# Global attention's transposes four blocks a bank in a row, the diagonal block last and copied with the others of its bank

## The chip, the cores and the metric

The kernel runs on one core of one Trainium2 chip, in one launch. The metric is the device time in microseconds of that core; lower is better. TensorE (PE) multiplies matrices, its weight loads are shown apart (PEld); VectorE (DVE), ScalarE (ACT) and GpSimd (POOL) work on elements; SyncE (SP) and ACT issue the transfers from memory here. TensorE writes its results to PSUM, which this kernel uses as eight banks of 128 x 512 single-precision values, and DVE or ACT copy them from there to the on-chip memory (SBUF) in which operands lie.

## The reference

Three layers follow each other, for 4 batches of 576 positions:

```python
# 1. attention of 8 heads (width 64) in a window of 64 positions
mask = (rel >= 0) & (rel < 64)
x = softmax(where(mask, q @ k.T / 8, -1e9)) @ v
# 2. four experts, each a causal attention of width 64 over all 576 positions
for e in range(4):
    q, k, v = x @ wq[e], x @ wk[e], x @ wv[e]
    a = softmax(where(causal, -1e9, q @ k.T / 8))
    out += weight_e * (a @ v @ wo[e])     # weight_e: softmax over the best 2 of 4 gates, else 0
# 3. mixing over positions, then over channels
theta = x @ w_theta
y = w_tok_r @ (x * cos(theta)) + w_tok_i @ (x * sin(theta))
u = x + y
return u + maximum(u @ w_ch, 0)
```

## The kernel before

The kernel is written as Python generators, one for each piece of work on a batch, and `merge` (line 45) interleaves them by costs from the table `KN` (line 27): at each turn the piece with the smallest share of its cost done goes on. That gives each instruction its rank. The framework's scheduler then sets the final order of each engine's queue, sets all waits, and lets buffers of a pool take turns. Each engine works its queue strictly in that order.

`phase_a` is the windowed attention (its tiles are `as`, `ams`, `apt`, `ao`). `qk` and `vg_gates` make the experts' queries, keys, values and gates (`qk`, `vg`). `attn(b, ep)`, line 403, is the global attention that the change touches: batch `b`, experts `2*ep` and `2*ep + 1` (a pair). `wo` projects its result (`x2`), `theta`, `mix` and `channel` are layer 3 (`th`, `xk`, `y`, `c`). Products are made of three matmuls each of split operands (`mm3`, lines 93 to 95).

`attn` takes five row tiles, t = 0 to 4; tile t has t full blocks of 128 columns and a diagonal block of 64 columns for each expert. For each expert of the pair:

- scores on TensorE into a bank `bs` (lines 432 and 434), mask and minimum on DVE (436), exp on ACT in place (441), sums and reciprocal on DVE (445, 446);
- scaling by DVE or POOL (453): the off-diagonal part in place in `pn` (traced as `bms`), the diagonal block into `pd` (`bpd`, both experts side by side).

Then, after a `yield`, TensorE transposes: off-diagonal blocks j = 0 .. t-1, for both experts each, two values of j (four transposes) a bank `bpt` (lines 458 to 464), and the diagonal block, both experts at once, in a bank of its own `bdt` (469, 470). Each bank is copied to `pT` (`bpT`) by ACT or DVE (466 and 468; 472 and 474). `KN["BC"]` = [1, 0, 1, 1] and `KN["BD"]` = [2, 1, 2, 1] choose the engine by batch. The products `o` read `pT`: off-diagonal ones from the last j down to 0 (480; traced at lines 145 and 148), the diagonal one with weights `VD` last (482). ACT and DVE split the result into `oh` and `ol` (483; traced at 87 and 90).

The banks `bpt`, `bdt` and `o` all come from `tbank` (line 399): two buffers that take turns (`tb`); in the last batch every third request goes to another bank (`ta`). A bank can be written again once all readers of its last tile are done. Over the five tiles a pair of experts asks for 1, 2, 2, 3 and 3 banks for transposes and one a tile for `o`, 16 in all.

Layers 1 and 2 of different batches run interleaved up to some 302 us; the middle of the span, from 64 us, is where the global attention runs.

Of the kernel before, what the change touches and what calls it, by code (L numbers as in the profile page):

```python
# [21 lines left out]
P = 128  # L22
# [35 lines left out]
def kernel(ctx, tc, qT, kT, vw, consts, w_in, w_o, w_th, w_tk, w_ch, outT):  # L58
    nc = tc.nc
# [5 lines left out]
    ident, ma1, ma0 = (cst[:, P * i : P * i + P] for i in range(3))  # L65
# [12 lines left out]
    def bank(shape, tag, name):  # L78
        return ps.tile(shape, F32, tag=tag, bufs=BANKS[tag], name=name)

    def pool_mul(out, in_, by):
        nc.gpsimd.tensor_scalar(out=out, in0=in_, scalar1=by, scalar2=1.0,  # L82
                                op0=ALU.mult, op1=ALU.mult)

    def split(dst_h, dst_l, src, eng_h, eng_l):
        if eng_h is nc.scalar:
            nc.scalar.copy(out=dst_h, in_=src)  # L87
        else:
            eng_h.tensor_copy(out=dst_h, in_=src)
        eng_l.tensor_sub(out=dst_l, in0=src, in1=f32(dst_h))  # L90
# [49 lines left out]
    def together():  # L140
        first = []

        def product(out, w, x, **flags):
            if not first:
                first.append(nc.tensor.matmul(out, w, x, **flags))
            else:
                with tc.issue_after(first[0].ins), tc.high_priority():
                    nc.tensor.matmul(out, w, x, **flags)

        yield product  # L150
# [29 lines left out]
    def sums(kind, tiles):  # L180
        nsum[kind] += 1
        return tiles[nsum[kind] % 4]
# [212 lines left out]
    def sbank(b, shape, name):  # L395
        ns[0] += 1
        return bank(shape, "as" if b == B - 1 and ns[0] % KN["SB"] == 0 else "bs", name)

    def tbank(b, shape, name):
        nt[0] += 1  # L400
        return bank(shape, "ta" if b == B - 1 and nt[0] % KN["TB"] == 0 else "tb", name)

    def attn(b, ep):
        vg, gw = VG[b], GW[b]
        for i in range(2):
            e = 2 * ep + i
            pool_mul(VD[ep][64 * i : 64 * i + 64, :, i, :], vg[0:64, :, e * D : (e + 1) * D], 1.0)
        oh = bp.tile([P, S], F32R, tag="oh", bufs=3, name=f"oh{b}{ep}")
        ol = bp.tile([P, S], F32R, tag="ol", bufs=3, name=f"ol{b}{ep}")
        O[b, ep] = (oh, ol)  # L410
        for t in range(5):
            w = QW[t]
            q0 = 0 if t == 0 else 64 + P * (t - 1)
            m = 64 if t == 0 else P
            mo = S - P if t == 0 else S - w
            if b == B - 1 and ep == 1 and t % 3 == 1:
                pn = rp.tile([P, 2, S], F32, tag="bmsx", name=f"bms{b}{ep}{t}")
            else:
                pn = bp.tile([P, 2, S], F32, tag="bms", bufs=2, name=f"bms{b}{ep}{t}")
            ss = sums(1, BS)  # L420
            sm = bp.tile([P, 2], F32, tag="bsm", bufs=4, name=f"bsm{b}{ep}{t}")
            pd = bp.tile([P, 2, 64], F32, tag="bpd", bufs=2, name=f"bpd{b}{ep}{t}")
            for i in range(2):
                e = 2 * ep + i
                n = f"{b}{e}{t}"
                qs, ka = QS[b, e], KA[b, e]
                ms = pn[:, i]
                cuts = [(0, w)] if w <= 512 else [(0, w // 2), (w // 2, w)]
                nm = bp.tile([P, 2], F32, tag="bnm", bufs=6, name=f"bnm{n}")
                for ci, (a, z) in enumerate(cuts):  # L430
                    s = sbank(b, [P, 512], f"bs{n}{a}")
                    nc.tensor.matmul(s[:m, : z - a], qs[:, q0 : q0 + m], ka[:, a:z],
                                     start=True, stop=False)
                    nc.tensor.matmul(s[:m, : z - a], qs[:, q0 : q0 + m], KL[e][:, a:z],  # L434
                                     start=False, stop=True)
                    nc.vector.tensor_tensor_reduce(  # L436
                        out=ms[:m, a:z], in0=s[:m, : z - a], in1=mb[:m, mo + a : mo + z],
                        scale=-0.125, scalar=nm[:m, 0:1] if ci else 3.0e38,
                        op0=ALU.add, op1=ALU.min, accum_out=nm[:m, ci : ci + 1],
                    )  # L440
                ex = nc.scalar.activation(out=ms[:m, :w], in_=ms[:m, :w], func=AF.Exp,  # L441
                                     bias=nm[:m, ci : ci + 1], scale=-1.0, accum_out=ss[:m, i, 0:1])
                if (b, ep, t, i) == (3, 1, KN["LT"], 1):
                    late[0] = ex
            nc.vector.tensor_reduce(out=sm[:m], in_=ss[:m], op=ALU.add, axis=AX.X)
            nc.vector.reciprocal(out=sm[:m], in_=sm[:m])
            for i in range(2):
                eng = nc.gpsimd if (False, i == 1 and t < 4, i == 1, t >= 2, i == 1 or t >= 3, True)[KN["SC"][2 * b + ep]] else nc.vector
                ms = pn[:, i]
                for dst, src in ((pd[:m, i], ms[:m, P * t : w]), (ms[:m, : P * t], ms[:m, : P * t])):  # L450
                    if src.shape[1] == 0:
                        continue
                    eng.tensor_scalar(out=dst, in0=src, scalar1=sm[:m, i : i + 1],
                                      scalar2=gw[:m, t, 2 * ep + i : 2 * ep + i + 1],
                                      op0=ALU.mult, op1=ALU.mult)
            yield 0.25 * (t + 1)
            pT = bp.tile([P, 5, 2, P], F32, tag="bpT", bufs=2, name=f"bpT{b}{ep}{t}")
            for j0 in range(0, t, 2):
                jn = min(2, t - j0)
                pt = tbank(b, [P, 2, 2, P], f"bpt{b}{ep}{t}{j0}")  # L460
                for jj in range(jn):
                    j = j0 + jj
                    for i in range(2):
                        nc.tensor.transpose(pt[:, jj, i, :], pn[:, i, P * j : P * j + P], ident)  # L464
                if (0, j0 == 2, t % 2, 1)[KN["BC"][b]]:
                    nc.vector.tensor_copy(out=pT[:, j0 : j0 + jn], in_=pt[:, :jn])
                else:
                    nc.scalar.copy(out=pT[:, j0 : j0 + jn], in_=pt[:, :jn])
            pt = tbank(b, [P, P], f"bdt{b}{ep}{t}")
            nc.tensor.transpose(pt[:, :m], pd[:m].rearrange("p h d -> p (h d)"), ident[:m, :m])  # L470
            if KN["BD"][b] == 0 or KN["BD"][b] == 1 and t % 2:
                nc.vector.tensor_copy(out=pT[:, t, 0, :m], in_=pt[:, :m])
            else:
                nc.scalar.copy(out=pT[:, t, 0, :m], in_=pt[:, :m])
            o = tbank(b, [P, P], f"o{b}{ep}{t}")
            for f in together():
                for j in reversed(range(t)):
                    for i in range(2):
                        e = 2 * ep + i
                        f(o[64 * i : 64 * i + 64, :m], vg[:, j, e * D : (e + 1) * D],  # L480
                          pT[:, j, i, :m], start=(j == t - 1), stop=False)
            nc.tensor.matmul(o[:, :m], VD[ep][:, t].rearrange("p h d -> p (h d)"), pT[:, t, 0, :m], start=(t == 0), stop=True)
            split(oh[:, q0 : q0 + m], ol[:, q0 : q0 + m], o[:, :m], nc.scalar, nc.vector)
            yield 0.4 * (t + 1)
# [169 lines left out]
    for i in range(2):  # L654
# [3 lines left out]
          (KN["CW"][5], load_w(w_in[:, W0:], NC, lambda c: wih[:, c, W0:], lambda c: wil[:, c, W0:], "bms")))  # L658
    for b in range(B):
        todo = [(KN["AT"][2 * b], attn(b, 0)), (KN["QK"][2 * b], qk(b, 1))]  # L660
        if KN["WOI"] == 2 * b:
            todo.append((KN["CW"][6], load_w(w_o, 2, lambda c: woh[c], lambda c: wol[c], "zc")))
# [16 lines left out]
        if b == 3:  # L679
# [4 lines left out]
            wkh += [kp.tile([P, S], F32R, name=f"wkh{c}") for c in range(NK0, 9)]  # L684
            wkl += [kp.tile([P, S], F32R, name=f"wkl{c}") for c in range(NK0, 9)]
        todo = [(KN["AT"][2 * b + 1], attn(b, 1))]
        if b < B - 1:
            todo += [(KN["QK"][2 * b + 1], qk(b + 1, 0)), (KN["VG"][b + 1], vg_gates(b + 1))]
# [88 lines left out]
```

## Time and profile before

| what | us |
|---|---|
| median of 3 runs | 528.98 (528.73 to 529.41) |
| the profiled execution | 528.16 |
| its span, from first to last instruction | 526.4 |
| TensorE busy | 506.6 |
| ACT busy | 329.6 |
| DVE busy | 323.1 |
| POOL busy | 304.6 |

The profile is of one execution. Busy time is time with an instruction of the program in work; for TensorE the ends of matmuls are modelled, so short waits between them can hide in it. The granted clock of TensorE is 1.00 (2.4 GHz) in every stretch. Rows name lines of the kernel and tiles without their numbers; `out<-in` are the tiles written and read, the shape after it partitions by elements, and a bracket shows how long the engine sat idle before, and what ended that.

### The profile page before, as it was taken

To read this page: it belongs to the slowest core of one execution; us is meant where nothing else is said; L and a number is where in the kernel's file an instruction comes from. 1 tells how busy PE (TensorE), PEld (TensorE's weight loads), DVE (VectorE), ACT (ScalarE), POOL (GpSimd) and SP (SyncE) were. 2 spreads that over 40 slices of the span, in tenths; PEclk is the share of its full clock that TensorE was granted. 3 is DMA by queue.
4 is the path that set the end of the run, shared out by engine and by line. 5 is a ranking of instruction groups with operands and counts; after the bars stand their busy time and mean duration, and the time that the engine had idled before them with its cause. 6 is when DMAs were issued, how large, how long until landed. Compare 5 with 4: busy or idle time off the path is not lost.

```text
span 526.4 us, 12343 instructions
## 1 busy us (share of the span) xinstructions
PE 506.6 (96%) x4372; PEld 475.5 (90%) x4372; DVE 323.1 (61%) x1244; ACT 329.6 (63%) x1045; POOL 304.6 (58%) x464
## 2 busy tenths in 40 slices
PE   8879999999999999999998999999999999999997
PEld 6669888899998998989787998999999999999997
DVE  5876887858778597558988787553325324533312
ACT  7977698866878768677788977551437136523410
POOL 5798789664848842247876676951475226531420
PEclk9999999999999999999999999999999999999999
DMA  7865224222314421112004121002000200011002
GB/s 248 253 185 169 97 60 147 64 67 92 103 34 134 142 76 32 32 29 73 37 2 159 62 82 42 1 0 80 12 2 1 68 24 1 1 57 35 1 1 91
DMA packets 21086, 36.80 MB, mean 70 GB/s; under 512 B 2336, under 2 KB 13600, under 8 KB 21024
## 3 DMA queue, kind: packets, MB, share of 16 engines
q1 hardware_dynamic: 19008, 31.22, 18.7%
q10 hardware_dynamic: 2016, 4.79, 2.7%
q8 instruction: 35, 0.57, 0.5%
q14 instruction: 27, 0.22, 0.2%
HBM read 31.28 MB, written 4.72 MB: 68 GB/s over the span
## 4 chain that ended last, share of the span: by engine, by line
PE 70%; DVE 11%; ACT 6%; POOL 6%; issue 3%; DMA 3%; ACTq 0%; POOLq 0%; DVEq 0%
PE y L95 6%; PE y L93 6%; PE y L94 6%; PE as L263 3%; PE c L95 3%; PE c L94 3%; PE c L93 3%; PE th L93 3%; PE th L95 3%; PE th L94 3%; PE bpt L464 2%; PE qk L93 2%; PE qk L95 2%; PE qk L94 2%; PE apt L288 2%
## 5 line engine op out<-in xcount | busy, mean ns | idle before, releaser
L90 POOL TENSOR_TENSOR z<-zf,z 128x256 fp32r<-128x256 f32 x72 | 52.9, 749 | 87.3 <-ACT z L87 86.9
L93 PE MATMUL y<-wkh,z 128*128 128x288 f32 x288 | 86.4, 301 | 0.5 <-DVE x2T L595 0.5
L94 PE MATMUL y<-wkl,z 128*128 128x288 f32 x288 | 85.3, 296 | 0.0
L95 PE MATMUL y<-wkh,z 128*128 128x288 f32 x288 | 84.7, 297 | 0.0
L276 ACT ACTIVATE ams<-ams,anm 128x128 f32<-128x128 f32 x144 | 56.6, 396 | 4.5 <-DVE anm L268 4.1
L93 PEld LDWEIGHTS y<-wkh,z 128*128 128x128 f32 x288 | 54.2, 188 | 1.4 <-DVE x2T L595 0.6
L94 PEld LDWEIGHTS y<-wkl,z 128*128 128x128 f32 x288 | 54.2, 188 | 0.0
L95 PEld LDWEIGHTS y<-wkh,z 128*128 128x128 f32 x288 | 53.9, 188 | 0.0
L283 POOL TENSOR_TENSOR ams<-ams,arc 128x384 f32<-128x384 f32 x48 | 40.8, 850 | 18.5 <-DVE arc L282 7.7
L87 ACT CAST z<-zf 128x256 fp32r<-128x256 f32 x72 | 27.6, 404 | 37.6 <-DVE zf L562 15.7
L441 ACT ACTIVATE bms<-bms,bnm 64x64 f32<-64x64 f32 (+4 forms) x80 | 45.0, 563 | 8.5 <-DVE bnm L436 7.9
L82 POOL TENSOR_SCALAR QD<-qt 64x192 f32<-64x192 f32 x72 | 39.6, 551 | 16.0 <-PE as L263 10.1
L562 DVE TENSOR_TENSOR zf<-xk,ang 128x256 f32<-128x256 f32 x64 | 25.4, 420 | 36.4 <-ACT ang L549 19.4
L547 ACT ACTIVATE ang<-ang 128x256 f32<-128x256 f32 x36 | 14.6, 416 | 51.9 <-DVE ang L546 51.8
L263 PE MATMUL as<-kt,QD 128*128 128x128 f32 x288 | 43.5, 288 | 3.1 <-ACT x0h L87 1.3
L263 PEld LDWEIGHTS as<-kt,QD 128*128 128x128 f32 x288 | 37.5, 197 | 6.8 <-ACT x0h L87 1.5
L268 DVE CUSTOM_DVE_ANT_0 ams<-as,cst 128x128 f32<-128x128 f32 x144 | 34.7, 283 | 6.3 <-PE as L263 3.1
L93 PE MATMUL th<-wth,cx 128*128 128x256 f32 x128 | 36.5, 285 | 2.1 <-DVE bnm L436 1.5
L436 DVE CUSTOM_DVE_ANT_0 bms<-bs,mb 64x64 f32<-64x64 f32 (+4 forms) x80 | 32.5, 423 | 9.3 <-PE bs L434 4.9
L94 PE MATMUL th<-wtl,cx 128*128 128x256 f32 x128 | 36.0, 281 | 0.0
L608 DVE SCALAR_TENSOR_TENSOR x2T<-c,x2T 128x288 f32<-128x288 f32 x32 | 14.5, 457 | 34.2 <-PE c L95 34.0
L95 PE MATMUL th<-wth,cx 128*128 128x256 f32 x128 | 35.4, 283 | 0.0
(198 smaller groups left out, 1742.3 us busy)
## 6 DMA issues: line engine op xcount, KB each, us to landing
vt<-in_dram SPq DMA_DIRECT2D x48, 192.0 KB, 3.1
kt<-in_dram SPq DMA_DIRECT2D x15, 320.0 KB, 3.0
qt<-in_dram SPq DMA_DIRECT2D x16, 288.0 KB, 3.2
out_dram<-x2T SPq DMA_DIRECT2D x32, 144.0 KB, 1.8
w64k<-in_dram SPq DMA_DIRECT2D x5, 576.0 KB, 3.7
w64k<-in_dram ACTq DMA_DIRECT2D x4, 576.0 KB, 3.7
w64t<-in_dram SPq DMA_DIRECT2D x4, 512.0 KB, 3.8
w64c<-in_dram ACTq DMA_DIRECT2D x8, 256.0 KB, 2.8
```

The source lines that it names most:

```text
L82: nc.gpsimd.tensor_scalar(out=out, in0=in_, scalar1=by, scalar2=1.0, op0=ALU.mult, op1=ALU.mult)
L87: nc.scalar.copy(out=dst_h, in_=src)
L90: eng_l.tensor_sub(out=dst_l, in0=src, in1=f32(dst_h))
L93: nc.tensor.matmul(out, wh, xh, start=first, stop=False)
L94: nc.tensor.matmul(out, wh, xl, start=False, stop=False)
L95: nc.tensor.matmul(out, wl, xh, start=False, stop=last)
L263: nc.tensor.matmul(s[:, i, :], QD[g][:, i], kt[:, 64 * blk : 64 * blk + 128], start=True, stop=True)
L268: nc.vector.tensor_tensor_reduce(out=ms[:, i, :], in0=s[:, i, :], in1=ma0 if (g == 0 and i == 0) else ma1, scale=-0.125, scalar=3.0e38, op ...
L276: nc.scalar.activation(out=ms[:, i, :], in_=ms[:, i, :], func=AF.Exp, bias=nm[:, i : i + 1], scale=-1.0, accum_out=sm[:, i, 0:1],)
L283: nc.gpsimd.tensor_mul(out=ms, in0=ms, in1=rc.unsqueeze(2).to_broadcast([P, 3, P]))
L436: nc.vector.tensor_tensor_reduce(out=ms[:m, a:z], in0=s[:m, : z - a], in1=mb[:m, mo + a : mo + z], scale=-0.125, scalar=nm[:m, 0:1] if ci ...
L441: ex = nc.scalar.activation(out=ms[:m, :w], in_=ms[:m, :w], func=AF.Exp, bias=nm[:m, ci : ci + 1], scale=-1.0, accum_out=ss[:m, i, 0:1])
```

## The change

The blocks of a tile are put in one list: (j, expert) for j = 0 .. t-1 and both experts, then the diagonal block (`None`). The list is cut into fours; each four is transposed into one bank and copied with one instruction. The diagonal block comes last: at t = 0, 2 and 4 it is alone in its bank as before, at t = 1 it follows two blocks, at t = 3 it stands third in the second bank. A bank that holds the diagonal block alone is copied by the engine of `BD`, every other by that of `BC`, with `j0 == 2` now written `k0 == 4`. A pair asks for 1, 1, 2, 2 and 3 banks for transposes, 14 with those of `o`.

```diff
                                       op0=ALU.mult, op1=ALU.mult)
             yield 0.25 * (t + 1)
             pT = bp.tile([P, 5, 2, P], F32, tag="bpT", bufs=2, name=f"bpT{b}{ep}{t}")
-            for j0 in range(0, t, 2):
-                jn = min(2, t - j0)
-                pt = tbank(b, [P, 2, 2, P], f"bpt{b}{ep}{t}{j0}")
-                for jj in range(jn):
-                    j = j0 + jj
-                    for i in range(2):
-                        nc.tensor.transpose(pt[:, jj, i, :], pn[:, i, P * j : P * j + P], ident)
-                if (0, j0 == 2, t % 2, 1)[KN["BC"][b]]:
-                    nc.vector.tensor_copy(out=pT[:, j0 : j0 + jn], in_=pt[:, :jn])
+
+            blocks = [(j, i) for j in range(t) for i in range(2)] + [None]
+            pf = pT.rearrange("p j i q -> p (j i) q")
+            for k0 in range(0, len(blocks), 4):
+                part = blocks[k0 : k0 + 4]
+                pt = tbank(b, [P, 4, P], f"bpt{b}{ep}{t}{k0}")
+                for k, blk in enumerate(part):
+                    if blk is None:
+                        nc.tensor.transpose(pt[:, k, :m], pd[:m].rearrange("p h d -> p (h d)"), ident[:m, :m])
+                    else:
+                        j, i = blk
+                        nc.tensor.transpose(pt[:, k, :], pn[:, i, P * j : P * j + P], ident)
+                if part == [None]:
+                    on_dve = KN["BD"][b] == 0 or KN["BD"][b] == 1 and t % 2
                 else:
-                    nc.scalar.copy(out=pT[:, j0 : j0 + jn], in_=pt[:, :jn])
-            pt = tbank(b, [P, P], f"bdt{b}{ep}{t}")
-            nc.tensor.transpose(pt[:, :m], pd[:m].rearrange("p h d -> p (h d)"), ident[:m, :m])
-            if KN["BD"][b] == 0 or KN["BD"][b] == 1 and t % 2:
-                nc.vector.tensor_copy(out=pT[:, t, 0, :m], in_=pt[:, :m])
-            else:
-                nc.scalar.copy(out=pT[:, t, 0, :m], in_=pt[:, :m])
+                    on_dve = (0, k0 == 4, t % 2, 1)[KN["BC"][b]]
+                (nc.vector.tensor_copy if on_dve else nc.scalar.copy)(
+                    out=pf[:, k0 : k0 + len(part), :m], in_=pt[:, : len(part), :m])
             o = tbank(b, [P, P], f"o{b}{ep}{t}")
             for f in together():
                 for j in reversed(range(t)):
```

In the rows below a name carries batch, pair and t, then a running number: `bpt2110` is the first transposes' bank of batch 2, pair 1, t = 1. Lines past 457 have shifted, so the transposes are now at 469 (off-diagonal) and 466 (diagonal), all copies at 474, the diagonal product at 483.

TensorE, batch 2, second pair, t = 1, before: transposes of the two blocks and of the diagonal one in two banks, then the products.

```order
L464 MATMUL bpt2110_3951<-cst_61,bms211_3929 128x128 x2
L470 MATMUL bdt211_3955<-cst_61,bpd211_3931 128x128
L288 MATMUL apt332_3781<-cst_61,ams332_3769 128x128 x3
L93 MATMUL vg32_4091<-wih_73,x1h_90 128x260
...
L95 MATMUL vg32_4091<-wih_73,x1l_91 128x260
L432 MATMUL bs2240_4066<-KA22_3282,QS22_3281 128x288
L434 MATMUL bs2240_4066<-KL2_126,QS22_3281 128x288
L145 MATMUL o211_3958<-bpT211_3950,vg2_2703 64x128
L148 MATMUL o211_3958<-bpT211_3950,vg2_2703 64x128
L482 MATMUL o211_3958<-bpT211_3950,VD1_123 128x128
L464 MATMUL bpt2120_3986<-cst_61,bms212_3964 128x128 x4
```

The same place now.

```order
L469 MATMUL bpt2110_3931<-cst_61,bms211_3909 128x128 x2
L466 MATMUL bpt2110_3931<-cst_61,bpd211_3911 128x128
L145 MATMUL ao330_3644<-apv330_3642,vt330_3618 64x64
L148 MATMUL ao330_3644<-apv330_3642,vt330_3618 64x64 x5
L148 MATMUL ao330_3644<-apv322_3604,vt322_3580 64x64 x6
L145 MATMUL o211_3936<-bpT211_3930,vg2_2691 64x128
L148 MATMUL o211_3936<-bpT211_3930,vg2_2691 64x128
L483 MATMUL o211_3936<-bpT211_3930,VD1_123 128x128
L432 MATMUL bs2240_4042<-KA22_3266,QS22_3265 128x288
L434 MATMUL bs2240_4042<-KL2_126,QS22_3265 128x288
L432 MATMUL bs224288_4046<-KA22_3266,QS22_3265 128x288
```

The three transposes share the bank `bpt2110`. Ahead of the first product stood products of the next batch (`vg32`), three transposes of the windowed attention (`apt332`) and a pair of score products (`bs2240`); now three rows of the windowed attention's small products (`ao330`) stand there, and the score products follow.

ACT, batch 0, first pair, t = 1, before: the copies to `bpT001` and what stands between them.

```order
L87 CAST oh00_999<-o000_1080 128x64
L468 COPY bpT001_1168<-bpt0010_1169 128x256
L276 ACTIVATE ams130_1278,AS2_106<-ams130_1278,anm130_1279 128x128 x3
L341 CAST KA03_1023<-qk031_1313 64x288
L441 ACTIVATE bms003_1358,BS0_108<-bms003_1358,bnm003_1361 128x448
L474 COPY bpT001_1168<-bdt001_1173 128x128
L135 ACTIVATE wth_66<-wtut0_1591 128x512
L87 CAST oh00_999<-o001_1176 128x128
```

The same place now.

```order
L87 CAST oh00_999<-o000_1080 128x64
L474 COPY bpT001_1168<-bpt0010_1169 128x384
L276 ACTIVATE ams130_1276,AS2_106<-ams130_1276,anm130_1277 128x128 x3
L341 CAST KA03_1023<-qk031_1311 64x288
L441 ACTIVATE bms003_1356,BS0_108<-bms003_1356,bnm003_1359 128x448
L87 CAST oh00_999<-o001_1174 128x128
L135 ACTIVATE wth_66<-wtut0_1587 128x512
```

One copy of 384 columns stands where that of 256 stood, the copy of 128 further down is gone, and the output copy `oh00` follows the exp.

In the whole order, products `qk` and `vg` for the next batch that stood between the first transposes of t = 0 and of t = 4 of batch 2's second pair are 83 before and 15 now; between the first transposes of that t = 4 and of batch 3 they are 13 before and 93 now.

## Rows read from the trace of the kernel before

**Rows 1.** The page: span; TensorE's busy time, share, instructions.

```profile
span 526.4 us, 12343 instructions
...
PE 506.6 (96%) x4372; PEld 475.5 (90%) x4372; DVE 323.1 (61%) x1244; ACT 329.6 (63%) x1045; POOL 304.6 (58%) x464
```

**Rows 2.** Busy by stretch: us, PE, PEld, DVE, ACT, POOL, clock, DMA.

```profile
64.00:224.06 160.06, 157.25 (x1552) 143.53 (x1551) 119.63 (x577) 124.90 (x451) 101.64 (x176) 1.00 0.27 85
224.06:244.21 20.15, 19.61 (x175) 17.71 (x175) 11.78 (x43) 15.20 (x42) 11.01 (x20) 1.00 0.11 31
244.21:252.90 8.69, 8.37 (x68) 7.28 (x66) 8.35 (x30) 6.69 (x20) 6.85 (x7) 1.00 0.39 136
252.90:302.00 49.10, 45.10 (x365) 40.04 (x364) 41.90 (x123) 41.53 (x112) 35.53 (x40) 1.00 0.18 60
350.00:526.40 176.40, 173.16 (x1342) 172.93 (x1340) 62.95 (x153) 60.27 (x150) 66.29 (x85) 1.00 0.08 28
```

**Rows 3.** The page, part 4: the chain that ended last, shares of the span.

```profile
PE 70%; DVE 11%; ACT 6%; POOL 6%; issue 3%; DMA 3%; ACTq 0%; POOLq 0%; DVEq 0%
```

**Rows 4.** By line and shape: copies, count | busy us, mean ns | idle before.

```profile
L293 ACT COPY apv<-apt 128x384 f32<-128x384 f32 x36 | 17.1, 476 | 6.0 <-PE apt L288 5.8
...
L474 ACT COPY bpT<-bdt 128x128 f32<-128x128 f32 x24 | 6.4, 267 | 0.8 <-PE bdt L470 0.6
...
L468 ACT COPY bpT<-bpt 128x256 f32<-128x256 f32 x10 | 3.8, 378 | 0.8 <-PE bpt L464 0.8
...
L291 DVE COPY apv<-apt 128x384 f32<-128x384 f32 x12 | 6.5, 542 | 0.3 <-PE apt L288 0.2
...
L466 DVE COPY bpT<-bpt 128x256 f32<-128x256 f32 x6 | 2.5, 420 | 0.9 <-PE bpt L464 0.9
L472 DVE COPY bpT<-bdt 128x128 f32<-128x128 f32 x8 | 2.2, 279 | 0.0
```

**Rows 5.** Long pieces of the chain, 64 to 302 us: start us, us, what.

```profile
153.89 0.48 ACT bpT L468
...
247.95 0.60 DVE bpT L466
```

**Rows 6.** Groups by line: weight loads of transposes and diagonal products.

```profile
L464 PEld LDWEIGHTS bpt<-cst,bms 128*128 128x128 f32 x160 | 19.2, 142 | 2.3 <-POOL bms L453 1.3 <-issue 0.5 <-PE o L482 0.3
...
L482 PEld LDWEIGHTS o<-bpT,VD 128*128 128x128 f32 x80 | 12.2, 189 | 2.2 <-issue 1.9 <-ACT wkh L132 0.2
...
L470 PEld LDWEIGHTS bdt<-cst,bpd 128*128 128x128 f32 (+1 forms) x40 | 5.6, 139 | 1.7 <-POOL VD L82 0.2 <-DVE ol L90 0.2 <-POOL bpd L453 0.2
```

**Rows 7.** Instructions on tile bpT: who waited for them (us, times).

```profile
  PEld o L145: 0.8, 3
...
  PE o L145: 0.2, 1
```

**Rows 8.** Timeline around 227 us, batch 2, second pair, t = 1 and 2.

```profile
226.44 0.38 PE L464 MATMUL bpt<-cst,bms 128*128 128x128 f32 x2
...
226.71 0.33 PE L470 MATMUL bdt<-cst,bpd 128*128 128x128 f32 x1
...
227.22 0.39 ACT L468 COPY bpT<-bpt 128x256 f32<-128x256 f32 x1
...
227.48 0.30 ACT L474 COPY bpT<-bdt 128x128 f32<-128x128 f32 x1
...
227.64 0.70 ACT L441 ACTIVATE bms<-bms,bnm 128x448 f32<-128x448 f32 x1
...
229.62 0.60 PE L464 MATMUL bpt<-cst,bms 128*128 128x128 f32 x4
```

**Rows 9.** Timeline around 248 us, the same pair, t = 4.

```profile
247.38 0.27 PE L470 MATMUL bdt<-cst,bpd 128*128 128x128 f32 x1
...
247.88 0.67 DVE L466 COPY bpT<-bpt 128x512 f32<-128x512 f32 x1
...
248.60 0.13 PEld L145 LDWEIGHTS o<-bpT,vg 128*64 128x64 f32 x1 [0.41 <-DVE bpT L466]
```

## The prediction, made before the changed kernel was run

> **What bounds the kernel now.** I read the page's busy shares first, then the busy times stage by stage, then the chain of waits, and last the rows of the copies that the change touches. The reader is to see in the shares that TensorE is busy for 506.6 us of a span of 526.4 [rows 1]. That is not one regime. From 350 us to the end it is busy for 173.16 of 176.40 us; in the attention between 64 and 302 us it is idle for 2.81, 0.54, 0.32 and 4.00 us in the four stretches shown, 7.7 us in all [rows 2]. Busy time of TensorE hides short waits, so the chain of waits has to be read too: over the whole span it runs through DVE for 11% and ACT for 6% [rows 3], which is 58 and 32 us. As the last 176 us are nearly all TensorE, nearly all of that lies in the first 350 us, so there the end moves by about 17 ns for 100 ns of DVE and by 9 ns for 100 ns of ACT. The change lives in the attention only: the first 64 us and the last 224 keep their work.
>
> The stretch from 224.06 us (second pair of batch 2) has DVE busy for 11.78 of 20.15 us; the next, up to 252.90, has it busy for 8.35 of 8.69 us, and after that TensorE stands for 4.00 of 49.10 us [rows 2]. So the kernel's slack sits around the passage from batch 2 to batch 3.
>
> **The change part by part.** *Copies.* Per batch and pair, steps t = 1 and t = 3 had a bank of two transposes and a bank of one, each with its copy; now one bank of three with one copy. That is 16 steps, 16 copies fewer. A copy of 128x384 from PSUM is in the trace on both engines, 476 ns on ACT and 542 on DVE [rows 4]. By the table that assigns the copies, ACT loses ten of 128x256 (378 ns) and eight of 128x128 (267 ns) and gets ten of 128x384: 3.78 + 2.14 - 4.76 = 1.16 us less. DVE loses six of 128x256 (420 ns) and eight of 128x128 (279 ns) and gets six of 128x384: 2.52 + 2.23 - 3.25 = 1.50 us less. Beside it lies TensorE's other work, so little of it reaches the end: by the chain's shares above 1.50 x 0.17 + 1.16 x 0.09 = 0.36 us. The ends are 0 (all hidden) and 2.66 us (all on the path). The rows say it is nearer to the first: of the transposes' copies only three stand among the long pieces of the chain between 64 and 302 us, of 0.48, 0.59 and 0.60 us (the first and the last in [rows 5]), and they are copies of 512 columns, which stay. I take 0.4 us gained.
>
> *The diagonal transposes and their bank.* TensorE does the same 160 and 40 transposes [rows 6]. What goes is a bank per odd step. The wait for a bank would show ahead of the diagonal transposes: of 1.7 us of idle weight-load time before them, 0.2 us was ended by DVE's second output copy, which frees a bank [rows 6]. Ahead of the other transposes POOL's scaling ends most of the 2.3 us. So fewer banks by themselves are worth between 0 and 0.2 us, and I count them at nothing; the cover is the rows of other work that stand between.
>
> *The products that read the copies.* All that waited visibly on the transposes' copies was the first attention product: 0.8 us on its weight load in three places, 0.2 us on its matmul [rows 7]. One of these, 0.41 us, is at t = 4 [rows 9], a step that keeps its copies. The diagonal product had 2.2 us before it, 1.9 of which nothing ended that the profile shows [rows 6]. So at most 0.6 us can go. Against it the first product of an odd step, which reads the last off-diagonal block, now waits for one more transpose (four in a row take 0.60 us with 0.27 us of the last one's own, so 0.11 us each [rows 8, 9]) and for 98 ns more of copy: 0.21 us later at 16 steps, 3.4 us if each shows. I take 0.2 us gained, with ends of 0.6 gained and 3.4 lost.
>
> *The order.* The scheduler places the whole attention anew, and this is the largest unknown. What the order shows at the second pair of batch 2: between the first transposes of t = 0 and of t = 4 stood 83 rows of products for the next batch (qk, vg), now 15; between t = 4 and the first transpose of batch 3 stood 13, now 93. Work that TensorE can always do moves out of a stretch in which ACT and DVE had room into the one in which DVE was 96% busy, and in front of the 4.00 us of standing. If it fills a sixth of the 0.32 + 4.00 us there, it is worth 0.7 us, which I take; the ends are all of the 4.3 us gained and as much lost, since what is moved away uncovers the first stretch.
>
> Sum: 0.4 + 0.2 + 0.7 = 1.3 us gained. The profiled execution took 528.16 us (526.4 of span and 1.76 around it), so it would take 526.86; the median of the runs is 528.98, 0.82 above the profiled one, and on that footing the forecast is 527.7 us.
>
> **A rule that speaks against it.** In the trace the bank of two and the bank of one could be read while the other was filled: at 227.22 and 227.48 us ACT copies the two in turn, while TensorE, done with both at 227.04, goes on [rows 8]. The Trainium skill, page "Perfetto Trace Analysis", section "Optimizing Tensor Performance", says that independent matmul groups should rotate through different PSUM banks, so that the copy of one runs beside the matmuls of the next. By that rule the change, which puts two groups in one bank, is a loss; what it would cost is the first rival below. This row does not bear the rule out for so small a group, as both copies came after both transposes.
>
> **Rivals.** *The product waits for the longer copy (slower).* At the second pair of batch 2, step 1, from the diagonal transpose (226.71 us) to the end of the second copy (227.78) took 1.07 us, with an exp of 0.70 us next on the queue [rows 8]. Between that transpose and the first product stood three transposes, nine vg products and a pair of score products; now only the small phase-A products. A first product that finds its copy unfinished waits like the one in rows 9, 0.41 us. If six of the 16 odd steps do, that is 2.5 us, less the 0.4 of the copies: 528.98 + 2.1 = 531.1 us. Three such steps cancel the gain of 1.3 us; more decide for the loss. For it: the order packs the three product rows closer behind the transposes at most odd steps. Against it: only 1.0 us of waits on these copies in 32 steps so far. The page's rule named above gives this case.
>
> *It is hidden anyway.* TensorE's work is the same, and ACT and DVE have room; then the order gives and takes alike, and the time is 528.9 us. For it: the idle time at stake is small beside 526.4 us. Against it: every instruction of the attention after 64 us has a new place.
>
> *The order alone decides, by more.* In batch 3 TensorE stands for 4.00 of 49.10 us. A better order takes three quarters of that (526.0 us), a worse one adds as much (532.0 us). For it: there is little other work there to cover a late product. Against it: both kernels do the same work in that stretch, with DVE busy for 41.90 us of it.
>
> **How the numbers follow.** About 0.2% (1.06 us) is what a measurement of this kernel can tell from no change. Small gain, between 526.3 and 527.9 us: 0.34, the likeliest, hence 527.7. The order gains more: 0.08. Hidden: 0.26. The product waits: 0.26. The order loses: 0.06. So faster 0.42, same 0.26, slower 0.32. The range must reach both signs: 524.5 (the third rival's 526.0 less half of the copies' 2.66, rounded down) to 532.0.
>
> **What would show it.** Copies: 72 instead of 88, those of 128x384 near 476 and 542 ns; if they are longer, the first term is smaller. Banks: no idle time ended by a bank's release ahead of the transposes. Products: waits ahead of the first attention product, by copies, stay under about 1 us in all; over 2.5 us the first rival has won. Order: the idle time of TensorE from the end of batch 2 to 302 us falls below 4.3 us. The prediction is wrong if the stretch up to the last attention step gets longer, or if the work after it, which the change does not name, moves the end.

## The result, and the profile after

The change makes the kernel slower: 533.12 us median of 5 runs (532.80 to 533.49), beside 528.98 us for the kernel before on the same chip (527.87 to 529.41). The ratio is 1.0081, with an interval of 1.0066 to 1.0096. The forecast was 527.7 us; the time lies outside its range.

The profiled execution took 532.80 us, 531.0 of it span. This is the page of the changed kernel: span, busy time of the engines, and the shares of the chain that ended last.

```profile
span 531.0 us, 12334 instructions
...
PE 507.7 (96%) x4372; PEld 475.5 (90%) x4372; DVE 325.3 (61%) x1236; ACT 329.8 (62%) x1037; POOL 303.1 (57%) x464
...
PE 65%; DVE 12%; ACT 10%; POOL 6%; DMA 4%; issue 3%; ACTq 0%; SPq 0%; POOLq 0%; DVEq 0%
```

TensorE has the same 4372 instructions as in [rows 1], DVE and ACT eight fewer each, yet the span is 4.6 us longer, and the chain that set the end runs through TensorE for 65% in place of the 70% of [rows 3]: more of the chain lies on ACT (10% for 6%) and DVE (12% for 11%).

The stretches of [rows 2], cut at the same events in the changed kernel (first transposes of batch 2's second pair, first of its last step, first of batch 3, to half a microsecond the end of the last diagonal product of batch 3, and 176.4 us before the end); the columns are as there.

```profile
64.00:223.65 159.65, 156.62 (x1529) 142.95 (x1527) 120.39 (x576) 123.96 (x443) 104.35 (x180) 1.00 0.27 86
223.65:235.87 12.22, 12.11 (x133) 10.21 (x132) 5.52 (x23) 8.04 (x24) 4.84 (x10) 1.00 0.01 2
235.87:257.30 21.43, 19.91 (x157) 18.12 (x153) 15.82 (x47) 15.23 (x39) 11.91 (x19) 1.00 0.26 84
257.30:308.10 50.80, 44.85 (x341) 38.19 (x341) 41.83 (x118) 41.00 (x107) 32.07 (x36) 0.97 0.17 58
354.60:531.00 176.40, 173.22 (x1342) 172.99 (x1340) 62.99 (x154) 60.61 (x151) 65.47 (x83) 1.00 0.08 28
```

The last step of the pair came 8.3 us earlier (235.87 for 244.21), the first transposes of batch 3 came 4.4 us later (257.30 for 252.90). TensorE's idle time in the four stretches of the attention was 7.7 us and is now 3.03 + 0.11 + 1.52 + 5.95 = 10.6 us, and a part of its busy time ran at a clock of 0.97. The last 176 us are the same work to 0.06 us.

The two stretches that tell most are fixed ones, 250 to 277 us and from there to 340. Before, then after:

```profile
250.00:277.00 27.00, 25.07 (x193) 21.55 (x192) 24.02 (x76) 21.63 (x64) 22.01 (x29) 1.00 0.05 19
277.00:340.00 63.00, 59.15 (x465) 55.55 (x464) 46.99 (x115) 48.03 (x126) 45.66 (x51) 1.00 0.22 72
```

```profile
250.00:277.00 27.00, 22.13 (x146) 18.51 (x144) 21.58 (x62) 20.14 (x54) 19.50 (x23) 0.94 0.14 45
277.00:340.00 63.00, 60.46 (x478) 55.84 (x479) 53.56 (x132) 49.97 (x137) 43.13 (x49) 1.00 0.21 72
```

In the first of them, the passage from batch 2 to batch 3, TensorE was busy for 25.07 of 27 us and did 193 rows; now 22.13 us, at a lower clock, and 146 rows. Laid beside each other at equal TensorE work, counted in columns of its matmuls and at times of the kernel before, the changed kernel is some 1.0 us late at 252 us (0.7 of it from before 64 us, in the part that does not change), 6.4 us late at 274 and 7.5 at 308, and gets 2.9 us back by 332, where the kernel before had waits of its own. From there the 4.7 us stay to the end.

The copies cost what was forecast. The new ones by shape (count | busy us, mean ns | idle before), answering to [rows 4]:

```profile
L474 ACT COPY bpT<-bpt 128x384 f32<-128x384 f32 x10 | 4.8, 480 | 0.4 <-PE bpt L466 0.3
...
L474 ACT COPY bpT<-bpt 128x128 f32<-128x128 f32 x16 | 4.2, 265 | 0.7 <-PE bpt L466 0.7
...
L474 DVE COPY bpT<-bpt 128x384 f32<-128x384 f32 x6 | 3.3, 547 | 0.5 <-PE bpt L466 0.5
```

480 and 547 ns, for 476 and 542 expected. With the copies of 128 columns that stay on ACT (16, 4.2 us), ACT's 10.2 us of [rows 4] became 9.0 and DVE's 4.7 became 3.3. DVE's busy time as a whole still rose, from 323.1 to 325.3 us: other instructions of DVE took longer, the scalings `bpd` among them (1.4 us in all). Who waited for the copied tile, answering to [rows 7] (us, times):

```profile
  PEld o L483: 0.8, 1
  PE o L483: 0.6, 1
  PEld o L145: 0.6, 3
```

The first products wait for copies 0.6 us in three places, where it was 0.8 us in three; new is one wait of the diagonal product (0.8 and 0.6 us are its weight load and its matmul, at 307.6 us), at the last step t = 4, whose copies the change leaves as they were. On the weight loads that is 1.4 us in all, more than the 1 us that the prediction named as its sign and less than the 2.5 us of the first rival. So by its own sign the rival of the longer copy does not hold.

What is late in the passage is seen in two small rows of DVE (start us, us, what): the last copy of batch 3's gates, and the first scaling that uses them. Before, then after:

```profile
244.67 0.16 DVE L388 COPY gw<-GX 64x4 f32<-64x4 f32 x1
...
250.96 1.20 DVE L453 TENSOR_SCALAR bpd<-bms,bsm,gw 64x64 f32<-64x64 f32 x1
```

```profile
249.86 0.16 DVE L388 COPY gw<-GX 64x4 f32<-64x4 f32 x1
...
254.54 0.60 DVE L453 TENSOR_SCALAR bpd<-bms,bsm,gw 64x64 f32<-64x64 f32 x1
```

The second pair of batch 2 ran ahead, and what batch 3 needs to begin (its V and gate products, which end at 244.0 us for 239.8) fell behind. Batch 3's attention then started 4 us later, with the pair's last step, which filled TensorE from 244 to 250 us before, already spent. This is what TensorE waited for between 250 and 277 us (us in total, times, longest); in the kernel before, all its waits there came to 1.8 us, none longer than 0.5:

```profile
PE bs L432 <- DVE bnm L436: 1.4, 3, 0.9
PE bpt L469 <- DVE bms L453: 1.4, 1, 1.4
PE x L93 <- DVE KL L342: 1.3, 1, 1.3
```

The first two, seen on the weight loads (the idle time ahead stands in brackets):

```profile
258.07 0.19 PEld L432 LDWEIGHTS bs<-KA,QS 128*128 128x128 f32 x1 [0.39 <-DVE bnm L436]
...
260.23 0.19 PEld L432 LDWEIGHTS bs<-KA,QS 128*128 128x128 f32 x1 [1.09 <-DVE bnm L436]
...
261.28 0.33 PEld L94 LDWEIGHTS qk<-x1l,wih 128*128 128x128 f32 x1
261.52 0.33 PEld L95 LDWEIGHTS qk<-x1h,wil 128*128 128x128 f32 x1
...
267.78 0.14 PEld L469 LDWEIGHTS bpt<-cst,bms 128*128 128x128 f32 x1 [1.60 <-ACT x2T L495]
```

The last row names ACT, which had long been done; the matmul behind it waited for the scaling of `bms` on DVE:

```profile
267.81 0.30 PE L469 MATMUL bpt<-cst,bms 128*128 128x128 f32 x1 [1.36 <-DVE bms L453]
```

DVE had the split of the next weights ahead of the step's sum and scaling. ACT's exp for that sum ended at 264.39 us, so some 1.2 us of the lateness is this place in DVE's queue, which has nothing to do with attention. The kernel before has such a split ahead of a sum too (253.97 to 256.24 us), so that alone is not new.

```profile
263.14 1.69 DVE L119 TENSOR_SCALAR wtuk<-wtuk 128x576 uint32<-128x576 uint32 x1 [0.22 <-ACT wtuk L117]
264.87 0.76 DVE L125 SCALAR_TENSOR_TENSOR wtuk<-w64k,wtuk 128x576 uint32<-128x576 uint32 x1
...
266.01 1.26 DVE L453 TENSOR_SCALAR bpd<-bms,bsm,gw 128x64 f32<-128x64 f32 x1
267.19 0.48 DVE L453 TENSOR_SCALAR bms<-bms,bsm,gw 128x384 f32<-128x384 f32 x1
```

Between the two waits, weight loads of one kind start 0.24 us apart at 261.28 and 261.52, where it was 0.13 us a little earlier (below); the record of the clock has a grant of 0.5 from 261.11 for 3.41 us.

```profile
255.93 0.19 PEld L94 LDWEIGHTS qk<-x1l,wih 128*128 128x128 f32 x1
256.06 0.19 PEld L95 LDWEIGHTS qk<-x1h,wil 128*128 128x128 f32 x1
```

### The profile page after: what moved, and what is told of

Read it like the earlier page. It is cut to its first block, busy times and chain, and to the rows that moved or that the text cites. A ratio compares the mean times of both kernels' runs of the same rounds, so it can differ in the third digit from the quotient of the medians.

```text
span 531.0 us, 12334 instructions
## 1 busy us (share of the span) xinstructions
PE 507.7 (96%) x4372; PEld 475.5 (90%) x4372; DVE 325.3 (61%) x1236; ACT 329.8 (62%) x1037; POOL 303.1 (57%) x464
## 4 chain that ended last, share of the span: by engine, by line
PE 65%; DVE 12%; ACT 10%; POOL 6%; DMA 4%; issue 3%; ACTq 0%; SPq 0%; POOLq 0%; DVEq 0%
PE y L93 7%; PE y L95 7%; PE y L94 7%; PE c L95 3%; PE c L94 3%; PE c L93 3%; PE as L263 3%; PE th L95 3%; PE th L94 3%; PE th L93 3%; PE bpt L469 2%; ACT ams L276 2%; DMA wst<-in_dram 2%; PE qk L93 2%; DVE bms L436 2%
## 5 line engine op out<-in xcount | busy, mean ns | idle before, releaser
L441 ACT ACTIVATE bms<-bms,bnm 128x576 f32<-128x576 f32 (+4 forms) x80 | 44.9, 561 | 12.3 <-DVE bnm L436 11.2
L263 PE MATMUL as<-kt,QD 128*128 128x128 f32 x288 | 42.1, 281 | 3.7 <-ACT x0h L87 1.3
```

Source lines behind the costliest of these rows:

```text
L263: nc.tensor.matmul(s[:, i, :], QD[g][:, i], kt[:, 64 * blk : 64 * blk + 128], start=True, stop=True)
```

## The experiments

The theory: the order at the passage from batch 2 to 3 makes the loss, not the copies and not the banks. Rivals: the longer copy or the shared bank makes it; the lowered clock makes it. Each kernel was timed against the kernel before on the same chip (medians of before 528.88, 529.03, 529.13 and 528.83 us for experiments 1 to 4, 5 to 8, 9 to 12, and 13 and 14). The table has the time, the ratio with its interval, and what TensorE was busy for in the two fixed stretches of the profiled execution, whose own time stands beside it where it is over 1 us from the median.

| kernel | us | ratio | 250-277 | 277-340 | sum |
|---|---|---|---|---|---|
| before | 528.98 | | 25.07 | 59.15 | 84.22 |
| after | 533.12 | 1.0081 [1.0066, 1.0096] | 22.13 | 60.46 | 82.58 |
| 1 change in batches 0-2 | 532.77 | 1.0071 [1.0055, 1.0086] | 22.59 | 59.84 | 82.44 |
| 2 change in batch 3 | 525.17 | 0.9930 [0.9915, 0.9945] | 25.49 | 61.66 | 87.15 |
| 3 after, held from t=2 | 528.28 (530.01) | 0.9991 [0.9980, 1.0002] | 22.85 | 61.77 | 84.62 |
| 4 after, held from t=3 | 528.59 (527.27) | 0.9996 [0.9980, 1.0011] | 22.78 | 61.78 | 84.57 |
| 5 after, nine fillers | 530.95 | 1.0038 [1.0019, 1.0058] | 23.23 | 60.25 | 83.48 |
| 6 before, order moved | 533.29 (531.09) | 1.0081 [1.0054, 1.0107] | 22.09 | 60.57 | 82.66 |
| 7 after, two copies | 531.39 | 1.0044 [1.0027, 1.0061] | 20.91 | 61.15 | 82.06 |
| 8 batch 3, two copies | 525.99 | 0.9950 [0.9936, 0.9965] | 25.41 | 60.36 | 85.77 |
| 9 batch 3, t=1 alone | 527.45 (525.79) | 0.9968 [0.9951, 0.9985] | 25.38 | 60.51 | 85.89 |
| 10 batch 3, t=3 alone | 525.91 | 0.9931 [0.9909, 0.9952] | 24.89 | 60.76 | 85.65 |
| 11 before, priority | 526.67 | 0.9951 [0.9932, 0.9970] | 24.85 | 60.36 | 85.22 |
| 12 batch 3, priority | 527.50 (526.36) | 0.9960 [0.9946, 0.9973] | 24.43 | 60.78 | 85.22 |
| 13 after, five fillers | 532.17 | 1.0062 [1.0038, 1.0086] | 22.82 | 60.45 | 83.27 |
| 14 after, six fillers | 530.91 | 1.0042 [1.0027, 1.0058] | 22.83 | 59.99 | 82.82 |

**Where: experiments 1 and 2.** The new code in some batches, the old in the others.

```diff
+            if b < 3:      # experiment 2: if b == 3
+                (new code)
+            else:
+                (old code)
```

> The change in batches 0 to 2 alone; batch 3 keeps its old banks and copies. Its TensorE order at the passage to batch 3 is that of the changed kernel (15 qk and vg products between t = 0 and t = 4 of batch 2's second pair, 93 behind). Order theory (the windowed attention of batch 3 falls behind the global attention of batch 2, so batch 3's gates and first scaling are late): 532 to 534 us, batch 3's first transpose at 256 to 258 us. Batch-3 theory (the new turn of banks and the merged copies of batch 3 cost it): 528.5 to 529.5 us. Wait theory (first products wait for longer copies, everywhere): three quarters of the loss, 532 us, but with waits on the copies over 2 us.

> The change in batch 3 alone; the order up to batch 3 is that of the kernel before (83 and 13). Order theory: 528 to 530 us, batch 3's first transpose near 253 us, no lowered clock. Batch-3 theory: 532 to 533.5 us. Wait theory: one quarter of the loss, 530 us.

Without any change in batch 3 the loss is there (532.77), and its passage looks like that of the changed kernel:

```profile
250.00:277.00 27.00, 22.59 (x146) 18.18 (x145) 23.68 (x66) 20.30 (x54) 20.17 (x23) 0.94 0.15 45
```

The change in batch 3 alone, which leaves the order up to the passage as it was, is 0.7% faster than before, which no theory expected. Its two stretches:

```profile
250.00:277.00 27.00, 25.49 (x196) 21.77 (x193) 23.19 (x78) 22.74 (x67) 23.36 (x30) 1.00 0.07 29
277.00:340.00 63.00, 61.66 (x491) 58.86 (x490) 47.34 (x119) 49.03 (x129) 46.48 (x51) 1.00 0.22 72
```

The passage is as full as before; the gain is in the second stretch, 61.66 us of TensorE for 59.15.

**Undoing the shift: experiments 3 and 4.** The changed kernel, with the off-diagonal transposes of batch 2's second pair held behind the last product of batch 3's windowed attention (`last_ao`; the lines that note it are left out).

```diff
-                        nc.tensor.transpose(pt[:, k, :], pn[:, i, P * j : P * j + P], ident)
+                        with tc.issue_after(last_ao[3].ins) if (b, ep) == (2, 1) and t >= 2 else ExitStack():   # 4: t >= 3
+                            nc.tensor.transpose(pt[:, k, :], pn[:, i, P * j : P * j + P], ident)
```

> The changed kernel with one edge more on TensorE's queue: the off-diagonal transposes of batch 2's second pair from t = 2 on stand behind the last product of batch 3's windowed attention. The order has 84 and 12 products at the passage, as before. All merged copies and banks stay. Order theory: 528 to 530 us, batch 3's first transpose near 253 us. Batch-3 theory and wait theory: 532 to 533.5 us as in the changed kernel.

> The same edge from t = 3 on only: 36 and 72 products at the passage, half of the shift. Order theory: between, 530 to 532 us, batch 3's first transpose at 254.5 to 256.5 us. The other theories: 532 to 533.5 us.

All banks and copies are those of the change, and the loss is gone: 528.28 and 528.59. But the passage did not fill up. Experiment 3:

```profile
250.00:277.00 27.00, 22.85 (x164) 19.51 (x163) 23.06 (x66) 19.93 (x53) 21.06 (x24) 0.94 0.14 45
277.00:340.00 63.00, 61.77 (x503) 58.92 (x502) 48.97 (x128) 50.53 (x138) 45.37 (x51) 1.00 0.21 72
```

It is still short of 2.2 us of TensorE's work there, at a lowered clock, and makes it up by a fuller second stretch. So the edge brings the time back, though not by the way that I had expected: batch 3's first transposes stand at 255.75 and 255.14 us, not near 253, and experiment 4, of which I had expected half of the loss back, has all of it. Nor does the edge of experiment 3 bring the gates back, nor much of the first scaling on DVE (POOL's first comes at 253.18, for 255.09 in the changed kernel and 252.11 before), and TensorE waits once for DVE's scaling for longer than in the changed kernel:

```profile
249.95 0.16 DVE L392 COPY gw<-GX 64x4 f32<-64x4 f32 x1
254.10 1.50 DVE L457 TENSOR_SCALAR bpd<-bms,bsm,gw 64x64 f32<-64x64 f32 x1
```

```profile
PE bpt L474 <- DVE bms L457: 2.7, 1, 2.7
```

So late gates and an emptier passage do not make the loss by themselves. (The profiled execution is the slowest of its twelve, 527.08 to 530.01 us.)

**Moving the order without the change: experiment 6.** The kernel before, with the V and gate products of batch 3's blocks 3 and 4 held behind the first transposes of the pair's last step.

```diff
+                with tc.issue_after(last_t4[(2, 1, 4, 0)].ins) if b == 3 and i >= 3 else ExitStack():
+                    mm3(g[:w], xh[:, c, i * P : i * P + w], ...)
...
-                        nc.tensor.transpose(pt[:, jj, i, :], pn[:, i, P * j : P * j + P], ident)
+                        last_t4[b, ep, t, j0] = nc.tensor.transpose(pt[:, jj, i, :], pn[:, i, P * j : P * j + P], ident)
```

> The kernel before with one edge: the projection products of V and of the gates of batch 3, blocks 3 and 4, may only stand behind the first transposes of the last step of batch 2's second pair. Banks, transposes and copies are all those of before; between the pair's first and last step stand 36 of batch 3's projection products in place of 83, and 72 in place of 13 behind (the changed kernel has 15 and 93). If the order at the passage makes the loss: slower than before, 530.5 to 533.5. If banks or copies make it: 528.9, within 0.5 of before.

It loses 0.8%, as the change does, with not one bank or copy changed. In the passage TensorE is as empty as in the changed kernel, but the waits are others (waited for, us in total, times, longest):

```profile
250.00:277.00 27.00, 22.09 (x157) 18.28 (x156) 20.94 (x70) 20.81 (x57) 23.41 (x28) 1.00 0.13 45
```

```profile
PE bs L435 <- POOL KA L82: 2.1, 2, 1.1
PE o L147 <- DVE ol L90: 0.9, 1, 0.9
PE bpt L467 <- POOL bms L456: 0.7, 1, 0.7
```

So a shift of this kind is enough for a loss of this size; that the very same waits make it is not shown. The profiled execution is the fastest of the six (531.09 to 535.17 us).

**Copies or banks: experiments 7 and 8.** The bank stays shared, the diagonal block is copied apart, in all batches (7) or in batch 3 alone (8).

```diff
+                cp = [(0, len(part), on_dve)]
+                if part[-1] is None and len(part) > 1:
+                    cp = [(0, len(part) - 1, on_dve), (len(part) - 1, len(part), KN["BD"][b] == 0 or KN["BD"][b] == 1 and t % 2)]
+                for c0, c1, dve in cp:
+                    (nc.vector.tensor_copy if dve else nc.scalar.copy)(
+                        out=pf[:, k0 + c0 : k0 + c1, :m], in_=pt[:, c0:c1, :m])
```

> The changed kernel with the bank still shared at t=1 and t=3, but the diagonal block copied apart from the others, on the engines of before. The order at the passage falls between the two kernels (36 projection products before the last step, 60 behind; before has 83 and 13, after 15 and 93). If the longer copies made the loss: back at about 529, within 0.5. If the shared bank made it by holding products back: as the changed kernel, 533. By the order theory it depends on the passage alone: 529 to 532.

> As the second run (the change in batch 3 alone, 525.17), but with the diagonal block at t=1 and t=3 copied apart from the others of its bank. The passage from batch 2 to 3 has the order of before, word for word. If the merged copies gave the gain of that run: back to 528.5-529.3. If the shared bank and the order that follows from it in batch 3 gave it: 524.5-527.

Experiment 7 lies in between (531.39), as its order does; its twelve executions spread from 528.75 to 533.36 us, and as copies and order both differ from the changed kernel's, it does not price the longer copy. In batch 3 alone the copies may be merged or not (525.17 and 525.99): the merged copy is not what gains there.

**Is the gain in batch 3 the bank's? Experiments 9 to 12.** 9 and 10 have the new code under `if b == 3 and t == 1` and `t == 3`; 11 and 12 wrap the second pair's step from the transposes to the last product, in the kernel before and in that of experiment 2:

```diff
+            with tc.high_priority() if (b, ep) == (2, 1) and t >= 1 else ExitStack():
```

> The change in batch 3 alone and there at t=1 alone (one shared bank fewer per pair, one merged copy of 384 columns). If the shared banks of batch 3 give the gain of 3.7 us step by step, the two steps share it: 526 to 528 here, and the gains of this run and the next add up to some 3.7. If it is the order of batch 3 that happens to come out better, the two runs don't add up, and each may lie between 525 and 529.5. The order moves 151 rows of TensorE against before (the change in the whole of batch 3 moved 169).

> The change in batch 3 alone and there at t=3 alone. As the run before this: 526 to 528 if banks give the gain step by step, so that both gains add up to some 3.7 us; no such sum if the order happens to come out better. 170 rows of TensorE moved against before.

> The kernel before with the transposes, copies and products of batch 2's second pair at a higher priority in the scheduler from t=1 on. Only 44 rows of TensorE move, by a few places; 83 projection products still stand between the pair's first and last step and 13 behind. If any change of the order were worth some per mille either way, this one is too: 526 to 532. If it takes a moved block of projection products to make the loss: 528.3 to 529.7.

> The change in batch 3 alone, with the priority of the run before this. If the gain of the change in batch 3 is the shared banks' own, it stays: 524 to 526. If it hangs on the order that came out there, it may go: 525 to 529.

The two steps gain 1.7 and 3.2 us, together 4.9 where both at once gained 3.7; by their intervals this difference could be noise. What decides is the priority: in the kernel before, with 44 rows of TensorE moved by a few places and no work changed, it gains 2.5 us, and with the change in batch 3, worth 3.7 us alone, both together gain only 1.6. So the change in batch 3 gains in one order and nothing in another, and a gain as large comes without it: it is one of the order. Of the two alternatives on record, that only a moved block of products counts (528.3 to 529.7) is out.

**The clock: experiments 5, 13 and 14.** Transposes of the identity into an unused slot of the bank, ahead of the score products that waited 1.09 us at 260.23 in the changed kernel. Nothing reads them.

```diff
+                if (b, ep, t) == (3, 0, 1):
+                    for _ in range(9):      # 13: range(5), 14: range(6)
+                        nc.tensor.transpose(pt[:, 3, :], cst[:, :P], ident)
```

> The changed kernel with nine more transposes of the identity, into the unused fourth slot of the bank of batch 3's first pair at t=1, in the place where TensorE stood idle for 1.09 us before 260.23; they compute nothing that is used. They cost about 9 x 0.13 = 1.2 us, nearly all inside that idle time. If the loss hangs in part on the lowered clock (granted 0.5 for 3.41 us from 261.11 in the changed kernel), the clock stays at 1.0 there and the time falls by 1 to 1.7 us, to 531.4-532.2. If the clock's fall is hidden by later slack, the clock stays at 1.0 and the time stays at 532.8-533.6. If the fall does not hang on this idle stretch, the granted clock falls all the same and the time is 533 to 534.

> The changed kernel with five filling transposes of the identity in the place of the nine of the fifth run, ahead of the score products that waited 1.09 us at 260.23. On every engine the order is that of the changed kernel, row for row, but for the five. If TensorE is busy enough with them for the clock to stay at 1.0, the slow stretch from 261.11 (3.41 us at half speed, some 1.7 us lost) goes, and if that is worth its full size at the end: 531.2 to 531.8; if later waits take it back: 532.5 to 533.5 with the clock at 1.0. If the clock falls all the same: 532.8 to 533.6.

> The same with six: here the scheduler moves the rows behind as with nine (3 rows differ from that kernel beside the fillers). If the clock's share is what the fifth run gained: as the run with five, when in both the clock stays at 1.0. If the moved rows gained it: 530.6 to 531.4 here, and the run with five stays at about 533.

With five, all other rows stand as in the changed kernel. The clock stayed at 1.00 in 261 to 265 us, where it had been 0.57 (changed kernel, then five fillers):

```profile
261.00:265.00 4.00, 4.00 (x21) 3.72 (x21) 3.68 (x6) 3.98 (x10) 1.43 (x1) 0.57 0.01 2
265.00:270.00 5.00, 3.42 (x26) 2.99 (x25) 4.17 (x13) 4.11 (x11) 4.03 (x5) 1.00 0.00 0
```

```profile
261.00:265.00 4.00, 3.39 (x26) 2.89 (x25) 3.65 (x6) 4.00 (x10) 1.41 (x1) 1.00 0.01 2
265.00:270.00 5.00, 2.69 (x11) 2.43 (x12) 3.70 (x13) 3.58 (x10) 4.59 (x6) 0.63 0.00 0
```

TensorE came sooner to the transposes that wait for the scaling, and stood there longer, 3.07 us for 1.60:

```profile
267.20 0.18 PEld L469 LDWEIGHTS bpt<-cst,bms 128*128 128x128 f32 x1 [3.07 <-ACT x2T L498]
```

After that wait the clock fell all the same, from 1.00 to 0.63 and then, in the row below, 0.78.

```profile
270.00:277.00 7.00, 7.00 (x56) 6.45 (x54) 3.32 (x13) 4.88 (x13) 5.76 (x8) 0.78 0.00 1
```

Of the 4.1 us of loss 1.0 was given back, less than the interval of that run resolves well (ratio 1.0062 [1.0038, 1.0086] for 1.0081 [1.0066, 1.0096]). With six and nine fillers the scheduler also moved some 25 rows of TensorE behind them, the granted clock stayed at 1.00 from 250 to 277 us, and the loss was 2.1 and 1.9 us. So the fall of the clock, kept away in one place, came in another, behind a longer wait.

How much of the loss is the clock's, these three do not settle, but the mean granted clock that is on record for each execution says something. In experiment 13, in the order of the changed kernel, the one execution that had the full clock throughout took 532.43 us, in the midst of the others (531.42 to 533.36); in experiment 14 the six with 0.999 or more had a median of 530.9 us, the five with 0.996 or 0.997 one of 530.8, and one with 0.994 took 534.07. That is a hint, the first from one execution alone, that the moved rows and not the clock gained there, one of the two cases that the expectation of experiment 14 names. In experiments 3 and 4 no execution had more than 0.997, and the loss is gone. In experiments 6 and 7 it is otherwise: the two executions of each with 0.999 or more took 531.09 and 531.71, and 528.75 and 529.10 us, all others 533.0 to 535.2, and 531.0 to 533.4. Whether there the fall costs the time or only comes with longer waits is open.

## Why the prediction was wrong

- *Copies (0.4 us gained).* The durations were right to 5 ns, DVE and ACT issue eight instructions fewer each, and by the rows above the copies take 1.2 us less on ACT and 1.4 us less on DVE (1.16 and 1.50 forecast). What that is worth at the end could not be isolated; in batch 3 two copies or one differ by 0.8 us, with other orders.
- *The diagonal transposes and their bank (nothing).* No wait of theirs for a bank stands out: 1.6 us of idle weight-load time before them, for 1.7 in [rows 6]. What I missed is that one bank fewer changes when the scheduler holds a step ready, and so the order far beyond the step: in experiment 7, with two copies as before and only the bank shared, the 83 and 13 products of the passage are 36 and 60.
- *The products that read the copies (0.2 us gained, up to 3.4 lost).* Right in size, but for the one new wait of 0.8 us at a step that the change leaves alone. The first rival is not borne out: 0.6 us of waits before the first products for 0.8, and the change in batch 3 alone, shared banks and all, is faster than before. The Trainium skill, page "Perfetto Trace Analysis", section "Optimizing Tensor Performance", has the rule that I weighed, that independent groups of matmuls should rotate through different banks. No run here shows a price for leaving it at groups of this size.
- *The order (0.7 us gained, ends of 4.3).* This is the step that failed, in sign and in size. I had the rows: 83 products to 15 and 13 to 93. From them I argued that movable work would fill the stretch in which DVE was 96% busy and the standing behind it. It did not: the idle time that was to fall below 4.3 us rose to 1.52 + 5.95 = 7.5 us. The products are not only filler: batch 3's gates and V come out of them, and batch 3's scaling waits for these. With them moved behind the start of the pair's last step the gates came 5.2 us and the first scaling 3.6 us later, and the step that had covered this wait was already spent. That the order makes the loss is shown (by experiment 6 without the change, by 3 and 4 with all of it and no loss); that it does so by the late gates is not: in experiment 3 they are as late (249.95 us for 249.86), and the loss is gone. The loss at the end, 4.6 us of span, is a little beyond the end that I had set, since I took it as bounded by the idle time there was (4.3 us): filler moved away can uncover waits that no idle time had shown.
- *The rivals.* "The order alone decides, by more" was the right mechanism, and I gave its loss 0.06. I placed it in batch 3 and priced it by idle time there (532.0). The runs put its origin before batch 3's own attention (experiment 1 has the loss with batch 3's code unchanged), and what it comes to in how well the stretch up to 340 us fills (experiments 3 and 4). What I had not weighed is that the order alone, at a few rows, moves this kernel by 0.5% (experiment 11), so that a gain of 0.6 us from the other terms could not carry a forecast.
- *What is still open.* By which waits the order makes the loss, and which of batch 3's late inputs counts, if any alone does; what the lowered clock adds; whether the weight splits ahead of the scaling on DVE (1.69 and 0.76 us) are the part that could be moved, which was not tried; and why experiments 3 and 4 fill the second stretch so well.

The version that beats both kernels is the change in batch 3 alone: 525.17 us, 0.7% below before. By experiments 11 and 12 that is an order that came out well, not a property of the shared bank.

## What to carry to other kernels

Where a scheduler places the work, price a small edit by the order that it brings, and look in that order for products that something else waits for: they are not free filler, however freely they can stand (here their lateness is seen, its price is not shown apart). Before a change is kept or thrown away, apply it stage by stage, and measure what a reordering without any change of work is worth: here 0.5%, or 2.5 us, more than the 0.4 us that I had set for the change's own copies.

## What the runs showed of the hardware

The granted clock of TensorE fell to half, 1.2 of 2.4 GHz, for 3.41 us in the changed kernel after TensorE had stood for 0.39 and then 1.09 us between 257.7 and 260.2 us; the weight loads of products of 288 columns then started 0.24 us apart in place of 0.13. With five more transposes in the second of these gaps it did not fall there, and fell behind a wait of 3.07 us instead. The kernel before, which stood for at most 0.7 us at a time in that passage, had no lowered clock in its profile; one wait of 1.7 us up to 281 us lowered none either. Nor did one of 2.10 us up to 266.17 us in experiment 14, so in these traces the length of one wait does not tell by itself whether the clock falls behind it. In the changed kernel DVE's shift of 576 columns (L119) took 0.45 us at 261.19, when POOL did nothing, and 1.69 us at 263.14, beside an instruction of POOL of 1.43 us from 263.09; that the one lengthens the other is not shown.
